# Turning attention outputs by row halves, ahead of the scores instead of behind the attend matmuls

## The chip, the cores and the metric

The kernel runs on one core of a Trainium2 chip. The metric is the device time of one execution in microseconds (us); the median of three runs of the kernel before is 767.42 us (766.53 to 768.09). Engines are named as in the profile: PE is the matmul engine (PEld its weight loads), DVE the vector engine, ACT the scalar engine, POOL the general engine, SP the engine that issues most DMAs.

## The reference: what is computed

Block-sparse attention, then a mixture of experts with one expert per token. Attention has 4 batches, 8 heads, 768 positions and a head size of 64; a mask by blocks of 32 allows neighbours, the first and last block and three sampled blocks per row.

```python
scores = scale * np.matmul(q, k.transpose(0, 1, 3, 2))        # scale = 1 / 8
scores = np.where(mask, scores, -1000000000.0)
attn = np.exp(scores - max); attn = attn / (sum + 1e-09)
out = np.matmul(attn, v)                                       # (4, 8, 768, 64)
x = out.transpose(0, 2, 1, 3).reshape(3072, 512)               # heads side by side
logits = x @ w_gate                                            # 8 experts
# each token goes to its expert of highest logit: y = relu(x @ w1[e]) @ w2[e]
# out = (probability of that expert) * y
```

## The kernel before, in words

**Pairs and steps.** The attention loop (L698) works on 16 pairs of heads; a pair is two heads of one batch, one head on partitions 0 to 63 and one on 64 to 127. Each pair has two steps, one per half of its 768 query rows (384 columns, `CW`, three groups of 128, `HC`), so 32 steps, numbered i from 0. The step (n, half) does, in this order:

- `load` (L87): DMAs of keys, queries and values of pair n+2, when half is 1.
- `turn` (L189): 12 transposes on PE of the keys (half 0) or queries (half 1) of pair n+1 into a PSUM buffer `tp`, and two copies by ACT.
- `scores` (L208), six times: matmuls L216 of keys by queries for both heads, each head from its own 64 partitions, into a PSUM buffer `s`; L219 adds the mask; ACT takes the exponential into `e` (L221); DVE adds the `e` up into `esum` (L227).
- `divide` (L245) for the step before, i-1: matmuls of `esum` by ones (L250, `sp`), ACT copies the sums to `ss` (L252), DVE takes reciprocals in three parts (L257) and multiplies the output `oT` of that step by them (L258).
- `attend` (L229), six times: matmuls L237 of values by `e` into `op`; at the end ACT copies `op` to `oT` (L242), still undivided, with head and dimension on the partitions and query rows on the columns.
- `rows_out` (L260), from n = 1 on, for the pair before, n-1, and the same half. That is the output of step i-2, divided in step i-1. It turns `oT` so that the rows come onto the partitions, and makes this pair's share of the logits, in one go: `oT` is the stationary operand of L270, and the moving one, `mix`, holds for each pair index an identity matrix with 8 columns of `w_gate` beside it (136 columns). Each group of 128 rows goes as two column halves of 64. ACT copies the PSUM tile `xr` to `xb` (L278), DVE adds the logits to `lgn` (L281 or L283), and after the second half SP writes the pair's 128 columns of x to DRAM, `x_rows` (L286). After the last pair of a batch, `gate` (L290) computes the probability of the best expert: DVE, one exponential on ACT, DVE, one small DMA.

From step 25 on, DVE also does the routing of the first three batches (`ranks`, `layout_a`, `one_hots`) and, in step 30, PE a few token matmuls (L593). After the loop come the last `divide`, then 28 expert tiles of two layers (L661, L676), each with its weights fetched by SP into two buffers and its rows gathered by POOL from `x_rows`. The outputs of the last pair are turned there: between the two groups of layer 1 of the first tile (half 0) and behind them (half 1).

**What sets the order.** PE, DVE and POOL run in the order in which the program is written (the manual schedule of L179, until L758). ACT and SP are ordered by the framework's planner. On each engine the work runs one after the other, with semaphores between engines. Buffers: `oT` four, `e` eight, `xb` two; in PSUM, `ps_s` has three buffers of two banks that `tp` and `s` use in turn, `ps_x` one bank for `xr` and `sp`, `ps_o` one for `op`.

Of the kernel before, what the change touches and what calls it, by code (L numbers as in the profile page):

```python
# [7 lines left out]
F32 = mybir.dt.float32  # L8
# [9 lines left out]
def kernel(  # L18
# [11 lines left out]
    nc = tc.nc  # L30
    P = 128
    B, H, S, D = q.shape
# [3 lines left out]
    NCH = S // P  # L36
    CW = NCH // 2 * P
    NPR = H // 2
    N, DM = out.shape
    E = moe_w_gate.shape[1]  # L40
# [17 lines left out]
    ident = const.tile([P, P], F32, name="ident")  # L58
# [4 lines left out]
    wg = const.tile([P, DB, E], F32, name="wg")  # L63
    lgn = const.tile([P, NT, E], F32, name="lgn")
    lmax = const.tile([P, NT], F32, name="lmax")

    x_d = nc.dram_tensor("x_rows", (N, XW), F32, kind="Internal").ap()


    mpool = ctx.enter_context(tc.tile_pool(name="mpool", bufs=1))  # L70
    ps_o = ctx.enter_context(tc.tile_pool(name="ps_o", bufs=1, space=PSUM))
    ps_x = ctx.enter_context(tc.tile_pool(name="ps_x", bufs=1, space=PSUM))

    upper, lent = {}, ExitStack()
# [9 lines left out]
    HC = NCH // 2  # L84
    loaded, turned = {}, {}

    def load(b, pr):  # L87
        got = []
        for src, nm in ((k, "k_sb"), (q, "q_sb")):
            t = ld.tile([P, NCH, 2, D], F32, name=nm)  # L90
            for hh in range(2):

                queue = nc.scalar if nm == "q_sb" and (b, pr) == (0, 0) else nc.sync
                queue.dma_start(t[:, :, hh, :], src[b, 2 * pr + hh].rearrange("(p c) d -> p c d", p=P))
            got.append(t)
        t = ld.tile([P, 2, NCH, D], F32, name="v_sb", bufs=3)
        nc.sync.dma_start(
            t.rearrange("p h c d -> p h (c d)"), v[b, 2 * pr : 2 * pr + 2].rearrange("h (p c) d -> p h (c d)", p=P),
        )
        got.append(t)  # L100
        loaded[(b, pr)] = got
# [2 lines left out]
    oh = mpool.tile([P, NCH, P], BF16, name="oh")  # L104
    pen = mpool.tile([P, S], BF16, name="pen")

    mix = mpool.tile([P, NPR, P + E], F32, name="mix")
    ones = mpool.tile([P, D], F32, name="ones")

    sums = mpool.tile([4 * B * NPR, CW], F32, name="sums")  # L110
# [58 lines left out]

    def make_mix():  # L170
        nc.scalar.dma_start(wg[:], moe_w_gate.rearrange("(c p) e -> p c e", p=P))
        nc.gpsimd.memset(mix[:], 0.0)
        for pr in range(NPR):
            nc.gpsimd.tensor_copy(mix[:, pr, :P], ident[:])
            nc.gpsimd.tensor_copy(mix[:, pr, P:], wg[:, pr, :])

    make_mask_pool = ExitStack()
    by_hand = ExitStack()
# [8 lines left out]
    xpool = ctx.enter_context(tc.tile_pool(name="xpool", bufs=2))  # L187

    def turn(b, pr, which):  # L189

        src = loaded[(b, pr)][which]
        dst = work.tile([P, S], F32, name="qT" if which else "kT")
        turned.setdefault((b, pr), {})[which] = dst
        tp = upper["ps_s"].tile([P, 2, 512], F32, name="tp", tag="s")

        for c in range(NCH):
            for j in range(2):
                r = slice(j * D, (j + 1) * D)
                nc.tensor.transpose(tp[:, j, c * D : (c + 1) * D], src[r, c].rearrange("p h d -> p (h d)"), ident[r, r])  # L199
        for j in range(2):  # L200
            nc.scalar.copy(  # L201
                dst.rearrange("p (c j t) -> p j c t", j=2, t=D)[:, j], tp[:, j, :CW].rearrange("p (c t) -> p c t", t=D),
            )

    rt = {}
    es, ops_, esums, xbs, s_alls = {}, {}, {}, {}, {}

    def scores(n, half, c):  # L208

        b, pr = pairs[n]  # L210
        kT, qT = turned[(b, pr)][0], turned[(b, pr)][1]
        cols = slice(half * CW, (half + 1) * CW)
        s = upper["ps_s"].tile([P, 2, 512], F32, name="s")
        for hh in range(2):
            r = slice(hh * D, (hh + 1) * D)
            nc.tensor.matmul(s[:, hh, :CW], lhsT=kT[r, c * P : (c + 1) * P], rhs=qT[r, cols], start=True, stop=False)  # L216
        for hh in range(2):
            r = slice(hh * D, (hh + 1) * D)
            nc.tensor.matmul(s[:, hh, :CW], lhsT=oh[r, c, :], rhs=pen[r, cols], start=False, stop=True)  # L219
        e = work.tile([P, 2, CW], F32, name="e", bufs=8)  # L220
        nc.scalar.activation(e[:], s[:, :, :CW], AF.Exp, scale=scale)  # L221
        es[(n, half, c)] = e
        if c == 1:
            esums[(n, half)] = work.tile([P, 2, CW], F32, name="esum")
        if c > 0:
            t = esums[(n, half)]
            nc.vector.tensor_add(t[:], es[(n, half, 0)][:] if c == 1 else t[:], e[:])  # L227
# [32 lines left out]
    def rows_out(n, half):  # L260

        b, pr = pairs[n]
        oT = ops_.pop((n, half))
        M = P + E
        xr = ps_x.tile([P, HC, M], F32, name="xr")

        M_ = D if n + 1 < len(pairs) else P
        for m in range(HC):
            for j in range(P // M_):
                nc.tensor.matmul(  # L270
                    xr[j * M_ : (j + 1) * M_, m, :], lhsT=oT[:, m * P + j * M_ : m * P + (j + 1) * M_], rhs=mix[:, pr, :],
                    start=True, stop=True,
                )
        if half == 0:
            xbs[n] = xpool.tile([P, NCH, M], F32, name="xb")
        xb = xbs[n]
        ms = slice(half * HC, (half + 1) * HC)
        nc.scalar.copy(xb[:, ms, :], xr[:])  # L278
        sofar = lgn[:, b * NCH + half * HC : b * NCH + (half + 1) * HC, :]
        if pr == 0:  # L280
            nc.vector.tensor_copy(sofar, xb[:, ms, P:])  # L281
        else:
            nc.vector.tensor_add(sofar, sofar, xb[:, ms, P:])  # L283
        if half == 1:
            rows = x_d[b * S : (b + 1) * S, pr * P : (pr + 1) * P]
            nc.sync.dma_start(rows.rearrange("(p c) w -> p c w", p=P), xb[:, :, :P])  # L286
            if pr == NPR - 1:
                gate(b)

    def gate(b):  # L290
        ts = slice(b * NCH, (b + 1) * NCH)
        nc.vector.reduce_max(lmax[:, ts], lgn[:, ts, :], axis=AX)
        ge = small.tile([P, NCH, E], F32, name="ge", bufs=2)
        nc.vector.tensor_tensor(
            ge[:], lgn[:, ts, :], lmax[:, ts].unsqueeze(2).to_broadcast([P, NCH, E]), op=ALU.subtract,
        )
        nc.scalar.activation(ge[:], ge[:], AF.Exp)
        gs = small.tile([P, NCH], F32, name="gs", bufs=2)
        nc.vector.reduce_sum(gs[:], ge[:], axis=AX)
        nc.vector.tensor_scalar_add(gs[:], gs[:], 1e-9)  # L300
        nc.vector.reciprocal(gs[:], gs[:])
        gw = small.tile([P, NCH, XW - DM], F32, name="gw", bufs=2)
        nc.vector.tensor_copy(gw[:], gs[:].unsqueeze(2).to_broadcast([P, NCH, XW - DM]))
        nc.sync.dma_start(x_d[b * S : (b + 1) * S, DM:].rearrange("(p c) w -> p c w", p=P), gw[:])

    pairs = [(b, pr) for b in range(B) for pr in range(NPR)]
# [141 lines left out]
    def count(ph):  # L448

        cps = bank(ph, [2, E])  # L450
        nc.tensor.matmul(cps[:, 0, :], lhsT=rt["lt"][:], rhs=rt["end" + ph][:], start=True, stop=True)
        nc.tensor.matmul(cps[:, 1, :], lhsT=rt["all"][:], rhs=rt["end" + ph][:], start=True, stop=True)
        cn = rt["cn" + ph] = sm.tile([P, 2, E], F32, name="cn" + ph)
        nc.vector.tensor_copy(cn[:], cps)
# [243 lines left out]
    for i, (n, half) in enumerate(steps):  # L698
        if half == 1 and n + 2 < len(pairs):
            load(*pairs[n + 2])  # L700
        if 0 < i and n + 1 < len(pairs):
            turn(*pairs[n + 1], half)
        for c in range(NCH):
            scores(n, half, c)
        if i == 0:
            make_mix()
        if i == 10:
            route_consts()
        if i > 0:
            divide(*steps[i - 1])  # L710
        for c in range(NCH):
            attend(n, half, c)
        if i == 0:
            turn(*pairs[1], 0)
        if n > 0:
            rows_out(n - 1, half)

        if (n, half) == (NA, 1):
            ranks("A", 0, TA)
        if (n, half) == (NA + 1, 0):  # L720
            count("A")
            layout_a()
            for i_ in range(2):
                fetch(i_, 1)
                fetch(i_, 2)
        if (n, half) == (NA + 1, 1):
            slots_a()
        if n == NA + 2:
            one_hots("A", rt["slA"], TA, KA, half)
        if (n, half) == (NA + 3, 0):  # L730
            tokens("A", TA, KA)
            for i_ in range(3):
                gather(i_)
        if n + 1 == len(pairs) and half == 1:
            turn_x(0)
# [92 lines left out]
```

## Time and profile before

| | us |
|---|---|
| median of three runs | 767.42 |
| the profiled execution's own time | 767.37 |
| its span, first to last instruction | 765.7 |
| start of the scores of step 0, step 1, step 2 | 10.65, 23.14, 33.23 |
| one step in the middle of the loop | 10.78 |
| end of the loop, start of the expert layers | 357.56 |

Busy time in the span: PE 749.5 us, weight loads 475.8, DVE 415.8, ACT 270.2, POOL 67.2. The step in the middle is the distance of two scores' starts in the chain of work that ended last (44.01 to 54.79). A line of the timeline gives the start in us, the busy time, the engine, the line of the kernel, the operation, `out<-in` with the program's names, the shapes, the number of instructions merged into it, and in brackets the idle time of the engine ahead of it and what ended that. Shapes such as 128*64 give rows by columns of the array that a matmul uses; a matmul of f32 shows as two instructions. Matmuls overlap in the pipeline, so the start of the next kind tells more than the end of the last. A line of the windows gives, for one stretch, each engine's busy time, then the TensorE clock granted (1.00 is full speed), the DMA share and GB/s.

### The profile page before, as it was taken

To read this page: it belongs to the slowest core of one execution; us is meant where nothing else is said; L and a number is where in the kernel's file an instruction comes from. 1 tells how busy PE (TensorE), PEld (TensorE's weight loads), DVE (VectorE), ACT (ScalarE), POOL (GpSimd) and SP (SyncE) were. 2 spreads that over 40 slices of the span, in tenths; PEclk is the share of its full clock that TensorE was granted. 3 is DMA by queue.
4 is the path that set the end of the run, shared out by engine and by line. 5 is a ranking of instruction groups with operands and counts; after the bars stand their busy time and mean duration, and the time that the engine had idled before them with its cause. 6 is when DMAs were issued, how large, how long until landed. Compare 5 with 4: busy or idle time off the path is not lost.

```text
span 765.7 us, 13053 instructions
## 1 busy us (share of the span) xinstructions
PE 749.5 (98%) x5134; PEld 475.8 (62%) x5134; DVE 415.8 (54%) x834; ACT 270.2 (35%) x425; POOL 67.2 (9%) x98
## 2 busy tenths in 40 slices
PE   7999999999999999999999999999999999999994
PEld 4555555555555555556777686786776776866682
DVE  4678777777778779997530235533434425323400
ACT  4666676667666675665111000100100100001000
POOL 4000000000000000002011121111111211211010
PEclk8999999999999999999999999999999999999998
DMA  8322333233322331842789989899899899899940
GB/s 187 83 60 48 82 84 85 63 83 84 85 56 51 83 84 44 319 165 78 244 308 333 344 311 348 320 329 346 320 329 362 314 344 345 320 346 339 355 147 6
DMA packets 119362, 157.57 MB, mean 206 GB/s; under 512 B 56499, under 2 KB 72947, under 8 KB 119284
## 3 DMA queue, kind: packets, MB, share of 16 engines
q1 hardware_dynamic: 112672, 142.42, 55.8%
q0 software_dynamic: 4480, 13.75, 4.6%
q8 instruction: 43, 0.70, 0.4%
q10 hardware_dynamic: 2132, 0.41, 0.3%
q14 instruction: 35, 0.29, 0.1%
HBM read 143.79 MB, written 13.73 MB: 206 GB/s over the span
## 4 chain that ended last, share of the span: by engine, by line
PE 86%; DMA 7%; issue 5%; another core or an unknown queue 0%; ACTq 0%; POOL 0%; ACT 0%; DVE 0%; POOLq 0%
PE hp L661 21%; PE zp L676 19%; PE s L216 17%; PE op L237 16%; DMA out_dram<-zo,sB 6%; PE s L219 4%; PE sp L250 3%; PE xr L270 3%; PE tp L199 2%; DMA q_sb<-in_q_dram 1%; PE tpg L650 0%; POOL xg L620 0%; ACT qT L201 0%; ACTq L117 0%
## 5 line engine op out<-in xcount | busy, mean ns | idle before, releaser
L661 PEld LDWEIGHTS hp<-xgT,w 128*128 128x128 f32 x1792 | 204.7, 192 | 12.6 <-issue 8.6
L661 PE MATMUL hp<-xgT,w 128*128 128x128 f32 x1792 | 205.6, 275 | 0.0
L676 PE MATMUL zp<-w,hT 128*128 128x512 f32 x448 | 196.9, 593 | 0.0
L642 DVE STREAM_TRANSPOSE xgT<-xg 32x128 f32<-32x128 f32 x352 | 106.5, 303 | 110.0 <-DMA xg<-x_rows,gB 94.0
L216 PE MATMUL s<-qT,kT 64*128 64x384 f32 x768 | 159.2, 493 | 0.9 <-ACT qT L201 0.9
L221 ACT ACTIVATE e<-s 128x768 f32<-128x768 f32 x192 | 152.4, 812 | 7.0 <-PE s L219 5.2
L676 PEld LDWEIGHTS zp<-w,hT 128*128 128x128 f32 x448 | 83.0, 190 | 94.2 <-issue 94.2
L227 DVE TENSOR_TENSOR esum<-esum,e 128x768 f32<-128x768 f32 x128 | 122.7, 958 | 14.6 <-ACT e L221 1.1
L237 PE MATMUL op<-e,v_sb 128*64 128x384 f32 x768 | 129.3, 486 | 0.0
L237 PEld LDWEIGHTS op<-e,v_sb 128*64 128x64 f32 x768 | 55.1, 137 | 68.8 <-issue 68.8
L216 PEld LDWEIGHTS s<-qT,kT 64*128 64x128 f32 x768 | 67.1, 190 | 38.4 <-issue 33.5
L257 DVE RECIPROCAL r<-ss 128x128 f32<-128x128 f32 x96 | 82.2, 912 | 1.3 <-ACT ss L252 1.3
L668 ACT ACTIVATE hT<-hp 128x512 f32<-128x512 f32 x33 | 19.7, 597 | 177.4 <-PE hp L661 174.4
L681 ACT ACTIVATE zo<-zp,xg 128x512 f32<-128x512 f32 x28 | 19.2, 687 | 176.7 <-PE zp L676 176.7
L666 DVE TENSOR_SCALAR hT<-hp 128x512 f32<-128x512 f32 x23 | 15.9, 692 | 101.4 <-issue 57.9
L227 DVE TENSOR_TENSOR esum<-e 128x768 f32<-128x768 f32 x32 | 30.6, 957 | 63.2 <-ACT e L221 63.2
L219 PE MATMUL s<-pen,oh 64*128 64x384 bf16 x384 | 63.2, 326 | 0.0
L242 ACT COPY oT<-op 128x384 f32<-128x384 f32 x32 | 15.3, 479 | 106.2 <-PE op L237 106.2
L682 POOL DMA_INDIRECT out_dram<-zo,sB x23 | 23.3, 1013 | 259.7 <-ACT zo L681 259.7
L219 PEld LDWEIGHTS <-oh 64*128 64x128 bf16 x384 | 18.9, 95 | 25.8 <-issue 0.9
L270 PEld LDWEIGHTS xr<-mix,oT 128*64 128x64 f32 (+1 forms) x372 | 24.0, 139 | 10.7 <-issue 10.7
L250 PE MATMUL sp<-esum,ones 128*64 128x384 f32 x128 | 27.7, 512 | 0.0
(174 smaller groups left out, 260.1 us busy)
## 6 DMA issues: line engine op xcount, KB each, us to landing
w<-in_moe_w_dram SPq DMA_DIRECT2D x56, 2048.0 KB
k_sb<-in_k_dram SPq DMA_DIRECT2D x32, 192.0 KB
v_sb<-in_v_dram SPq DMA_DIRECT2D x16, 384.0 KB
x_rows<-xb SPq DMA_DIRECT2D x16, 384.0 KB
q_sb<-in_q_dram SPq DMA_DIRECT2D x30, 192.0 KB
sums<-ss SPq DMA_DIRECT2D x32, 3.0 KB
q_sb<-in_q_dram ACTq DMA_DIRECT2D x2, 192.0 KB
xg<-x_rows,gB POOLq DMA_INDIRECT x23, 7.5
```

What stands on the lines that cost most here:

```text
L216: nc.tensor.matmul(s[:, hh, :CW], lhsT=kT[r, c * P : (c + 1) * P], rhs=qT[r, cols], start=True, stop=False)
L219: nc.tensor.matmul(s[:, hh, :CW], lhsT=oh[r, c, :], rhs=pen[r, cols], start=False, stop=True)
L221: nc.scalar.activation(e[:], s[:, :, :CW], AF.Exp, scale=scale)
L227: nc.vector.tensor_add(t[:], es[(n, half, 0)][:] if c == 1 else t[:], e[:])
L237: nc.tensor.matmul(op[hh * D : (hh + 1) * D, :], lhsT=v_sb[:, hh, c, :], rhs=e[:, hh, :], start=(c == 0), stop=(c == NCH - 1),)
L250: nc.tensor.matmul(sp[hh * D : (hh + 1) * D, :], lhsT=ones[:], rhs=esum[:, hh, :], start=True, stop=True)
L257: nc.vector.reciprocal(r[:, m * P : (m + 1) * P], ss[:, m * P : (m + 1) * P])
L270: nc.tensor.matmul(xr[j * M_ : (j + 1) * M_, m, :], lhsT=oT[:, m * P + j * M_ : m * P + (j + 1) * M_], rhs=mix[:, pr, :], start=True, stop ...
L642: nc.vector.transpose(xT[d, :, t], xg[t, :DM].rearrange("p (c q) -> p c q", c=DB)[:, :, d])
L661: nc.tensor.matmul(hp[:, m, :], lhsT=st[i]["w1"][:, c, fb * P : (fb + 1) * P], rhs=st[i]["xT"][:, c, :], start=(c == 0), stop=(c == DB - 1),)
L676: nc.tensor.matmul(zp[:], lhsT=st[i]["hT"][:, fb, :], rhs=st[i]["w2"][:, fb, :], start=(fb == 0), stop=(fb == FB - 1),)
L682: ins = nc.gpsimd.indirect_dma_start(out=out[:, :], out_offset=bass.IndirectOffsetOnAxis(ap=of("s", i, P), axis=0), in_=zo[:], in_offset=N ...
```

## The change

`rows_out` moves from the end of step (n, half) to its start, ahead of `turn` and the scores; it still serves pair n-1 and the same half. For all pairs but the last, L270 is split by row halves: for each group of 128 rows and each head, 64 partitions of `oT` (one head) times 64 partitions of a smaller `mix` (64x64 identity and that head's 64 rows of `w_gate`, 72 columns). The two heads write to two banks of a `ps_s` buffer, `xr2`. ACT copies it in one instruction (432 elements per partition instead of 408). The logits now come in two shares, added by two DVE instructions, and the rows go to DRAM by two DMAs per pair, one per head, with pieces of 64 numbers instead of 128. The last pair keeps its place in the expert layers, whole groups of 128 columns and a table of its own, `mix2`. `make_mix` fills the smaller tables.

```diff
     def make_mix():
         nc.scalar.dma_start(wg[:], moe_w_gate.rearrange("(c p) e -> p c e", p=P))
-        nc.gpsimd.memset(mix[:], 0.0)
         for pr in range(NPR):
-            nc.gpsimd.tensor_copy(mix[:, pr, :P], ident[:])
-            nc.gpsimd.tensor_copy(mix[:, pr, P:], wg[:, pr, :])
+            for hh in range(2):
+                r = slice(hh * D, (hh + 1) * D)
+                nc.gpsimd.tensor_copy(mix[r, pr, :D], ident[r, r])
+            nc.gpsimd.tensor_copy(mix[:, pr, D:], wg[:, pr, :])
+        nc.gpsimd.tensor_copy(mix2[:, :P], ident[:])
+        nc.gpsimd.tensor_copy(mix2[:, P:], wg[:, NPR - 1, :])
...
+            W = D + E
+            xr = upper["ps_s"].tile([P, 2, 512], F32, name="xr2", tag="s")
+            for m in range(HC):
+                for hh in range(2):
+                    r = slice(hh * D, (hh + 1) * D)
+                    nc.tensor.matmul(
+                        xr[:, hh, m * W : (m + 1) * W], lhsT=oT[r, m * P : (m + 1) * P], rhs=mix[r, pr, :], start=True, stop=True,
+                    )
+            xb = xbs[n].rearrange("p (h c w) -> p h c w", h=2, c=NCH)
+            nc.scalar.copy(xb[:, :, ms, :], xr[:, :, : HC * W].rearrange("p h (c w) -> p h c w", c=HC))
+            for hh in range(2):
+                part = xb[:, hh, ms, D:]
+                if pr == 0 and hh == 0:
+                    nc.vector.tensor_copy(sofar, part)
+                else:
+                    nc.vector.tensor_add(sofar, sofar, part)
+                if half == 1:
+                    nc.sync.dma_start(dest[:, :, hh * D : (hh + 1) * D], xb[:, hh, :, :D])
...
     for i, (n, half) in enumerate(steps):
         if half == 1 and n + 2 < len(pairs):
             load(*pairs[n + 2])
+
+        if n > 0:
+            rows_out(n - 1, half)
         if 0 < i and n + 1 < len(pairs):
             turn(*pairs[n + 1], half)
         for c in range(NCH):
...
             attend(n, half, c)
         if i == 0:
             turn(*pairs[1], 0)
-        if n > 0:
-            rows_out(n - 1, half)
```

More of the change, by code (lines that the diff above doesn't have):

```diff
@@ L105 @@
     pen = mpool.tile([P, S], BF16, name="pen")
-    mix = mpool.tile([P, NPR, P + E], F32, name="mix")
+    mix = mpool.tile([P, NPR, D + E], F32, name="mix")
+    mix2 = mpool.tile([P, P + E], F32, name="mix2")
     ones = mpool.tile([P, D], F32, name="ones")
@@ L263, in rows_out @@
         oT = ops_.pop((n, half))
[L264 to L273, printed above, removed]
-        if half == 0:
-            xbs[n] = xpool.tile([P, NCH, M], F32, name="xb")
@@ L276, in rows_out @@
[L276 to L281, printed above, removed]
-        else:
-            nc.vector.tensor_add(sofar, sofar, xb[:, ms, P:])
+        ms = slice(half * HC, (half + 1) * HC)
+        sofar = lgn[:, b * NCH + half * HC : b * NCH + (half + 1) * HC, :]
+        if half == 0:
+            xbs[n] = xpool.tile([P, 2 * NCH * (D + E)], F32, name="xb")
@@ new lines, in rows_out @@
+        dest = x_d[b * S : (b + 1) * S, pr * P : (pr + 1) * P].rearrange("(p c) w -> p c w", p=P)
+        if n + 1 == len(pairs):
+            xr = ps_x.tile([P, HC, P + E], F32, name="xr")
+            for m in range(HC):
+                nc.tensor.matmul(xr[:, m, :], lhsT=oT[:, m * P : (m + 1) * P], rhs=mix2[:], start=True, stop=True)
+            xb = xbs[n][:, : NCH * (P + E)].rearrange("p (c w) -> p c w", c=NCH)
+            nc.scalar.copy(xb[:, ms, :], xr[:])
+            nc.vector.tensor_add(sofar, sofar, xb[:, ms, P:])
+            if half == 1:
+                nc.sync.dma_start(dest, xb[:, :, :P])
+        else:
+            W = D + E
+            xr = upper["ps_s"].tile([P, 2, 512], F32, name="xr2", tag="s")
+            for m in range(HC):
+                for hh in range(2):
[11 more added lines that the diff above has]
+                    nc.vector.tensor_add(sofar, sofar, part)
+                if half == 1:
+                    nc.sync.dma_start(dest[:, :, hh * D : (hh + 1) * D], xb[:, hh, :, :D])
@@ L284, in rows_out @@
         if half == 1:
-            rows = x_d[b * S : (b + 1) * S, pr * P : (pr + 1) * P]
-            nc.sync.dma_start(rows.rearrange("(p c) w -> p c w", p=P), xb[:, :, :P])
             if pr == NPR - 1:
```

## The prediction, made before the result was known

> **What bounds the kernel now.** I read the chain of work that ended last first, then the timeline of one step of the attention loop by engine, then the waits.
>
> ```profile
> PE 86%; DMA 7%; issue 5%; another core or an unknown queue 0%; ACTq 0%; POOL 0%; ACT 0%; DVE 0%; POOLq 0%
> ```
>
> The chain runs on PE almost throughout: any time in which PE stands still in the attention loop is added to the end. The loop has 32 steps, one about every 10.78 us. Here is PE in step 11 (its scores begin at 130.11) and at the seam to step 12 (140.89), then two rows of the weight loads:
>
> ```profile
> 130.11 0.86 PE L216 MATMUL s<-qT,kT 64*128 64x384 f32 x4
> ...
> 135.10 0.87 PE L250 MATMUL sp<-esum,ones 128*64 128x384 f32 x4
> 135.80 4.04 PE L237 MATMUL op<-e,v_sb 128*64 128x384 f32 x24
> 139.67 0.86 PE L270 MATMUL xr<-mix,oT 128*64 128x136 f32 x12
> 140.47 0.58 PE L199 MATMUL tp<-ident,k_sb 64*128 64x64 f32 x12
> 140.89 0.86 PE L216 MATMUL s<-qT,kT 64*128 64x384 f32 x4
> ```
> ```profile
> 140.46 0.45 PEld L199 LDWEIGHTS tp<-ident,k_sb 64*128 64x128 f32 x12 [0.18 <-issue]
> ...
> 141.59 0.35 PEld L216 LDWEIGHTS s<-qT,kT 64*128 64x128 f32 x4 [0.23 <-issue]
> ```
>
> PE goes from one kind to the next without a hole: scores 4.99 us (130.11 to 135.10), sums 0.70, attend 3.87, outputs 0.80, turned keys 0.42; together 10.78. Now DVE and ACT over the same stretch:
>
> ```profile
> 130.17 0.56 DVE L258 TENSOR_TENSOR oT<-oT,r 128x384 f32<-128x384 f32 x1
> ...
> 132.89 0.96 DVE L227 TENSOR_TENSOR esum<-e 128x768 f32<-128x768 f32 x1 [2.07 <-ACT e L221]
> 133.95 4.15 DVE L227 TENSOR_TENSOR esum<-esum,e 128x768 f32<-128x768 f32 x4
> 138.01 2.57 DVE L257 RECIPROCAL r<-ss 128x128 f32<-128x128 f32 x3
> 140.62 0.56 DVE L258 TENSOR_TENSOR oT<-oT,r 128x384 f32<-128x384 f32 x1
> ```
> ```profile
> 131.24 4.79 ACT L221 ACTIVATE e<-s 128x768 f32<-128x768 f32 x6
> 136.02 0.49 ACT L252 ACTIVATE ss<-sp 128x384 f32<-128x384 f32 x1
> 139.89 0.48 ACT L242 COPY oT<-op 128x384 f32<-128x384 f32 x1 [3.38 <-PE op L237]
> 140.58 0.50 ACT L278 COPY xb<-xr 128x408 f32<-128x408 f32 x1 [0.22 <-PE xr L270]
> 141.09 0.86 ACT L201 COPY kT<-tp 128x384 f32<-128x384 f32 x2
> ```
>
> The multiply of L258 in this step ends at 140.62 + 0.56 = 141.18. It divides the output of step 10 (divide is called for the step before). The matmuls of L270 at 139.67 don't need it: they turn the output of step 9, divided at 130.17 + 0.56 = 130.73, which gives 8.9 us of room. That room is why PE never waits for a division:
>
> ```profile
> PEld xr L270 <- issue: 10.7, 60, 0.2
> ```
>
> In the list of waits this is the only entry of L270: never DVE.
>
> **Which output is turned at a seam.** Step i ends with rows_out of step i-2 before the change. After it, step i begins with rows_out of step i-2. Nothing lies on PE between the end of one step and the start of the next, so PE does the same kinds in the same order (attend, outputs, turned keys, scores); but the output that is turned is one step younger. At the seam of 139.67 it is that of step 10, whose multiply ends at 141.18. The stationary operand of the new matmul is oT, so the first weight load of xr2 waits: PE could begin at 139.67 and may begin at 141.18. Behind that load stand the 12 transposes of the keys and all scores of the next step; ACT has nothing to exponentiate and DVE nothing to add until they come.
>
> **The new length of a step.** With PE waiting for DVE, DVE for ACT and ACT for PE, the step is a loop, which I walk from the first exponential (e0).
> - e0 to the end of the multiply: 131.24 to 141.18 = 9.94 us (two exponentials, five adds at 1.03 to 1.06, three reciprocals, the multiply). The division before the change goes through the same: nothing here is touched.
> - End of the multiply to the first weight load: I take 0.05, from ACT's copy ending at 141.95 and its next one beginning 0.01 later at the one end, and 0.2 (the "issue" gap of the L270 row) at the other.
> - Weight load to first matmul: 0.16 (L216: 141.59 in the loads, 141.75 on PE).
> - First output matmul to the next e0, as it is now: 139.67 to 141.09 + 0.86 = 141.95, so 2.28.
> - What the new shape changes in that: 12 matmuls stream 72 columns instead of 136, but load 64x128 weights instead of 128x64. No row shows this pair. By streaming alone the 0.69 of the chain's xr piece would fall by 72/136 to 0.37; by the loads of the transposes (12 of the same size in 0.45 us) also about 0.4; by L216's (four in 0.35 us, each about 0.19, two row halves beside each other, so about 0.115 per pair) 6 x 0.115 = 0.69. L216's is the nearest row, a full f32 multiply from the same halves, so I take 0.69: no change. ACT's copy has 432 elements instead of 408, by 479 ns for 384 and 499 for 408 about 0.02 more; the last, shorter matmul ends 0.05 earlier. Together 2.26.
>
> Sum: 9.94 + 0.05 + 0.16 + 2.26 = 12.41 us, against 10.78: **1.63 us more per step**.
>
> **The whole loop.** Step 2 is the first with a turned output at its start. Step 1 had none on PE, so there the matmuls themselves are new as well: the multiply of step 1 ends at 34.18 and the exponentials of step 2 began at 34.13.
>
> ```profile
> 33.62 0.56 DVE L258 TENSOR_TENSOR oT<-oT,r 128x384 f32<-128x384 f32 x1
> ```
>
> e0 of step 2 moves to 34.18 + 2.47 = 36.65, 2.5 us later. Steps 3 to 29 are 27 times 1.63 = 44.0. Steps 30 and 31 have no keys to turn; there e0 waits for the first scores, not for ACT's copies, and the old steps were 10.35 and 10.95 (the second holds 0.6 of token matmuls, which now lie in the stall); I estimate 1.6 and 1.0. Step 31 no longer ends with an output: 0.79 back (xr at 355.23, the next transposes at 356.02). 2.5 + 44.0 + 2.6 - 0.8 = 48.3. The gate of a batch (DVE, ACT, DVE: its exponential stood between the two key copies and made e0 0.15 us late unnoticed) falls into the loop three times: 0.6. Sum 48.9.
>
> **What is hidden.** One more add of logits per step (0.18) lies in DVE's idle time ahead of the next exponentials (2.07 now, some 3.7 then); uncovered it would be 30 x 0.2 = 6. The new tables are 14 copies on POOL (64x64 or 128x8, at most 0.29 each, so 4 us once) instead of a memset and 8 copies, more than 10 us ahead of their first use. The 15 further row transfers take SP 0.59 each; the bytes are the same in pieces half as long. SP's key loads behind them are issued some 40 us (141.78 against a turn at about 183) ahead of need, so I charge nothing, at worst 15 x 0.59 = 9 if SP were the bound. One xr2 buffer more goes round in the three of ps_s: the second scores of a step need its copy, which ends 0.86 ahead of e0. The routing work on DVE (up to 2.4 us after a multiply in steps 25 to 29) fits ahead of the next e1, which comes 4.1 us after it. The second half, from 357 us on, only starts later. It streams its weights through two buffers, so a longer loop prefetches nothing more.
>
> **The clock.** PE will stand for about 1.4 us in each step. The only holes that this trace shows are ahead of 10.65 us, the longest 2.6 us, and the clock fell after them:
>
> ```profile
> 8.00:10.00 2.00, 1.20 (x22) 0.90 (x18) 0.84 (x2) 1.12 (x3) 0.89 (x6) 0.71 1.37 216
> ...
> 14.00:16.00 2.00, 2.00 (x12) 1.08 (x12) 0.90 (x1) 0.96 (x2) 0.00 (x0) 0.58 1.27 222
> ```
>
> The seventh figure is the granted clock: 0.71 means half speed from 8.84, 0.58 until 15.68, so 6.8 us. [...] No row here has a hole of 1.4 us at full clock, so it stays a rival.
>
> **The rivals.** (1) *Not slower*: DVE divides ahead of its adds. The sums are copied at 136.02 + 0.49 = 136.51; three reciprocals and the multiply behind that end at 139.7, just when PE arrives. Then there is no wait, and the time is 767 if the matmuls cost the same, 757 if they fall from 0.69 to 0.37 (30 x 0.32). It decides from the point where the multiply ends 1.5 us earlier in the step. Against it: DVE takes its work in the written order in this step, the first reciprocal coming only after the fifth add although its input was there 1.5 us before. That the turned output in effect stays where it was, because the order isn't what I read, would give 767 too. (2) *The clock falls at each stall.* At half speed outputs and keys take 1.1 more and two rounds of scores 1.6 more (0.81 now), so about 3 us per step: 30 x 3 on top is about 906; at some stalls only, from 840 up. (3) *Dear loads*: the two row halves don't load beside each other. L661 loads 32 full weights in 3.57 us, 0.111 each; 12 x 0.111 = 1.33 instead of 0.69, which is 30 x 0.64 = 19 more: 836. At the other end the transposes' loads give 30 x 0.27 = 8 less: 808.
>
> **How the numbers follow.** The profiled execution took 767.37 (its span 765.7 and 1.7 around it), the median is 767.42: 767.4 + 48.9 = **816**. Forecast 0.85 (803 to 832: loads, wake-up 0.05 to 0.2, DVE's further add). Dear loads 0.03, the clock 0.07, not slower 0.05, of it 0.03 faster and 0.02 the same. The range 803 to 834 leaves out the clock and the not slower case and most of the dear loads. Faster, same and slower by over 0.2%, about what a measurement of this kernel can tell from no change: 0.03, 0.02, 0.95.
>
> **What would show it.** Right: a wait of PEld at xr2 for DVE's oT, some 30 times with about 1.5 us each; steps of 12.4 us; DVE's idle time ahead of esum up by 1.6; clock 1.0 throughout; xr2 about 0.7 long, and the second half as long as before. Wrong: no such wait (rival 1), slices at a lower clock (rival 2), an xr2 stretch of 0.4 or 1.3 us (loads).

## The result and the profile after

The changed kernel takes 814.25 us (median of 6 runs, 813.52 to 814.85) against 767.23 in the same runs before: a ratio of 1.0612, interval 1.0598 to 1.0626. The prediction was 816, in a range of 803 to 834. The profiled execution has a span of 811.8 us, 46.1 more than before; the expert layers start at 403.7 us instead of 357.6, so all of it lies ahead of them, in the attention loop.

The chain of work that ended last, by engine, of the changed kernel:

```profile
PE 50%; DVE 22%; issue 16%; DMA 6%; ACT 4%; POOL 1%; another core or an unknown queue 0%; DVEq 0%; POOLq 0%
```

DVE had 0% of it before and now has 22%, PE 50% instead of 86%. The waits of the changed kernel (waiter, what it waited for: total us, times, longest):

```profile
PEld xr L290 <- issue: 58.5, 28, 2.3
...
PE xr L290 <- DVE oT L262: 38.1, 27, 1.7
```

This is the seam, the join of two steps on PE: 27 times PE waits 1.41 us, and what ends the wait is the multiply. The weight loads' own row names no releaser ("issue"); it counts the time since the last load of attend. (The three other seams wait as well, 0.7, 1.4 and 1.4 us, and name a routing instruction of DVE that stands behind the multiply.) One seam by engine; line numbers are 4 to 20 higher than before:

```profile
151.82 4.04 PE L241 MATMUL op<-e,v_sb 128*64 128x384 f32 x24
157.28 0.89 PE L290 MATMUL xr<-mix,oT 64*128 64x72 f32 x12 [1.42 <-DVE oT L262]
157.97 0.57 PE L203 MATMUL tp<-ident,k_sb 64*128 64x64 f32 x12
158.34 0.90 PE L220 MATMUL s<-qT,kT 64*128 64x384 f32 x4
```
```profile
157.25 0.78 PEld L290 LDWEIGHTS xr<-mix,oT 64*128 64x128 f32 x12 [2.06 <-issue]
```
```profile
153.97 2.57 DVE L261 RECIPROCAL r<-ss 128x128 f32<-128x128 f32 x3
156.57 0.56 DVE L262 TENSOR_TENSOR oT<-oT,r 128x384 f32<-128x384 f32 x1
158.76 0.40 DVE L300 TENSOR_TENSOR lgn<-lgn,xb 128x24 f32<-128x24 f32 x2 [1.63 <-ACT xb L294]
```
```profile
147.19 4.85 ACT L225 ACTIVATE e<-s 128x768 f32<-128x768 f32 x6
...
158.20 0.52 ACT L294 COPY xb<-xr 128x432 f32<-128x432 f32 x1 [1.82 <-PE xr L290]
158.62 0.87 ACT L205 COPY kT<-tp 128x384 f32<-128x384 f32 x2
159.44 4.85 ACT L225 ACTIVATE e<-s 128x768 f32<-128x768 f32 x6
```

The multiply ends at 157.13, PE's first matmul follows at 157.28, and a step, from one e0 (147.19) to the next (159.44), is 12.25 us. DVE, which PE waits for, then stands idle itself for 1.63 us, until ACT has copied the outputs: the engines wait for each other in a ring.

Two steps were longer than the others, 13.8 and 13.6 us. Windows of the changed kernel over step 9 and step 10 (busy time of PE, PEld, DVE, ACT, POOL, then the granted clock, DMA share, GB/s):

```profile
119.80:132.20 12.40, 10.73 (x92) 5.92 (x90) 9.37 (x17) 6.77 (x13) 0.00 (x0) 1.00 0.43 99
132.30:146.10 13.80, 12.47 (x94) 6.74 (x91) 8.36 (x13) 7.00 (x12) 1.11 (x7) 0.88 0.13 31
```

A clock of 0.88 over 13.8 us is half speed for 3.3 us. In the profiled execution it happened at two seams of 30.

### The profile page after: what moved, and what is told of

It is laid out like the page before. It is cut to its first block, busy times and chain, and to the rows that moved or that the text cites. A ratio compares the mean times of both kernels' runs of the same rounds, so it can differ in the third digit from the quotient of the medians.

```text
span 811.8 us, 13112 instructions
## 1 busy us (share of the span) xinstructions
PE 753.6 (93%) x5134; PEld 487.0 (60%) x5134; DVE 422.0 (52%) x864; ACT 267.1 (33%) x425; POOL 66.9 (8%) x103
## 4 chain that ended last, share of the span: by engine, by line
PE 50%; DVE 22%; issue 16%; DMA 6%; ACT 4%; POOL 1%; another core or an unknown queue 0%; DVEq 0%; POOLq 0%
PE hp L678 14%; PE s L220 13%; PE zp L693 13%; DVE esum L231 10%; DVE r L261 9%; DMA out_dram<-zo,sB 6%; PE xr L290 3%; ACT e L225 3%; PE s L223 3%; DVE oT L262 2%; PE tp L203 1%; PE op L241 1%; POOL xg L637 1%; DVE allow L152 0%; PE tpg L667 0%
## 5 line engine op out<-in xcount | busy, mean ns | idle before, releaser
L220 PE MATMUL s<-qT,kT 64*128 64x384 f32 x768 | 162.0, 498 | 1.1 <-ACT qT L205 1.1
L220 PEld LDWEIGHTS s<-qT,kT 64*128 64x128 f32 x768 | 74.0, 192 | 33.6 <-issue 29.4
L223 PE MATMUL s<-pen,oh 64*128 64x384 bf16 x384 | 69.4, 327 | 0.0
L290 PE MATMUL xr<-mix,oT 64*128 64x72 f32 x360 | 26.9, 279 | 41.6 <-DVE oT L262 38.1
L290 PEld LDWEIGHTS xr<-mix,oT 64*128 64x128 f32 x360 | 23.4, 187 | 59.6 <-issue 58.5
L223 PEld LDWEIGHTS <-oh 64*128 64x128 bf16 x384 | 25.1, 96 | 20.4 <-issue 1.6
```

Of the source, the lines that this page charges most:

```text
L290: nc.tensor.matmul(xr[:, hh, m * W : (m + 1) * W], lhsT=oT[r, m * P : (m + 1) * P], rhs=mix[r, pr, :], start=True, stop=True,)
```

## The experiments

Each changes one thing of the changed kernel (of the kernel before, for e2; e5 also changes the number of two buffers). Ratios are to runs of the kernel before on the same chip, at 767.28 us for e1 to e4 and 766.84 for e5 to e8.

**e1: the shape without the place.**

```diff
-        if n > 0:
-            rows_out(n - 1, half)
         if 0 < i and n + 1 < len(pairs):
...
         if i == 0:
             turn(*pairs[1], 0)
+        if n > 0:
+            rows_out(n - 1, half)
```

> The new shape alone: row halves, xr2 in ps_s, two row DMAs per pair, two logit adds, but rows_out at the end of the step as before the change, so that a seam turns the output that is one step older. Theory (the whole loss is PE waiting for the multiply of an output that is one step too young): no wait of xr2 for DVE, steps of 10.7 to 10.8 us, 764 to 770 in all. Rival (the shape costs: 128-column loads, the shared ring of ps_s, the longer ACT copy, shorter DMA pieces): 775 or more, up to 814 if it is all of it.

Measured: 767.09 us, ratio 0.9996 (0.9987 to 1.0005); steps of 10.76 us, no wait of xr2 for DVE. The shape is neutral where it is.

**e2: the place without the shape.** The same move of two lines made in the kernel before.

> The new place alone: the kernel before with rows_out moved to the start of the step, whole 128-column identity, ps_x buffer, one row DMA. Theory: the same wait of about 1.4 us at each of 30 seams, steps of 12.2 to 12.4 us, 810 to 819 in all. Rival (the shape costs): under 790.

Measured: 817.2 us, ratio 1.0652 (1.0636 to 1.0669); steps of 12.43 us. Its waits:

```profile
PE xr L270 <- DVE oT L258: 38.5, 27, 1.7
```

The place alone is the whole loss, and a little more. With the new shape a waiting step is 0.18 us shorter; 0.15 of it lies in ACT's copies, where xb to e0 took 159.96 to 161.35 here and 158.20 to 159.44 in the changed kernel.

**e3: divide ahead of the scores.** Place and shape stay.

```diff
+        if i > 0:
+            divide(*steps[i - 1])
         for c in range(NCH):
             scores(n, half, c)
...
-        if i > 0:
-            divide(*steps[i - 1])
         for c in range(NCH):
             attend(n, half, c)
```

> The changed kernel with divide of the step before called ahead of the scores instead of behind them, so that DVE's reciprocals and multiply come before the five adds and are done some 5 us before the next seam. Place and shape stay those of the change. Theory: the wait is gone; PE changes between row and column halves twice more per step, each about 0.1 us by the seams of before: 766 to 776. Rival (the buffers, ACT's order of copies or the shape hold PE at the seam): 800 or more.

Measured: 783.08 us, ratio 1.0211 (1.0196 to 1.0227). The regular wait is gone, as expected, but the total missed by 7. Steps are 11.05 us, not 10.76, and one step had a hole of 3.7 us on PE; the scores behind it took 1.49 to 1.65 us a round instead of 0.81. PE's row and ACT's row name that hole's cause:

```profile
339.63 1.65 PE L220 MATMUL s<-qT,kT 64*128 64x384 f32 x4 [3.71 <-ACT e L225]
```
```profile
338.38 0.49 ACT L256 ACTIVATE ss<-sp 128x384 f32<-128x384 f32 x1 [4.93 <-DMA sums<-ss]
```

The small DMA of the sums (3 KB) took 9.35 us, from 328.95 to 338.30, and held an `ss` buffer until then. In the execution before the change, where four loads of expert weights of 2 MB each are issued from 308.28 to 313.08, the DMA engines' busy share is 1.03 from 313 to 330 us, and the same DMA held ACT for 1.7 us; DVE's reciprocals waited 1.3 us for it and PE not at all. That the loads held it up in e3 too is my reading.

**e5: divide first in the step**, so that the sums' matmuls lie between attend and the outputs.

```diff
-            oT = work.tile([P, CW], F32, name="oT", bufs=4)
+            oT = work.tile([P, CW], F32, name="oT", bufs=3)
...
-        ss = work.tile([P, CW], F32, name="ss")
+        ss = work.tile([P, CW], F32, name="ss", bufs=3)
...
+        if i > 0:
+            divide(*steps[i - 1])
         if n > 0:
             rows_out(n - 1, half)
...
-        if i > 0:
-            divide(*steps[i - 1])
         for c in range(NCH):
             attend(n, half, c)
```

> The changed kernel with divide of the step before called first of all in the step, so that PE's order at a seam is attend, sums, outputs, keys, scores: the reciprocals come ahead of the adds as in the kernel that divides ahead of the scores, but the sums' matmuls (column halves) stand next to the attend matmuls (column halves). Three buffers for ss and three for oT instead of two and four, so that a late sums DMA can't hold ACT. Theory (in the kernel that divides ahead of the scores, the 0.29 us left per step came from its two further changes between row and column halves, and its one hole of 3.7 us from the sums DMA): steps of 10.7 to 10.8 us, no hole in the loop, 765 to 771. Rival (the 0.29 is the sums' matmuls or ACT's longer list at the seam): steps of 11.0 or more, 775 to 785.

Measured: 774.40 us, ratio 1.0094 (1.0078 to 1.0109). Steps are 10.76 us, so e3's 0.29 went with the two further changes between column and row halves (in neither kernel does PE wait in such a step). The total missed by 3: the three steps with a gate took 12.2 to 12.4, and those with routing on DVE about 11.5. DVE, ACT and PE at a gate:

```profile
109.73 2.58 DVE L261 RECIPROCAL r<-ss 128x128 f32<-128x128 f32 x3 [2.09 <-ACT ss L256]
112.42 0.56 DVE L262 TENSOR_TENSOR oT<-oT,r 128x384 f32<-128x384 f32 x1
...
113.56 0.21 DVE L311 TENSOR_TENSOR ge<-lgn,lmax 128x48 f32<-128x48 f32 x1
...
114.85 0.95 DVE L231 TENSOR_TENSOR esum<-e 128x768 f32<-128x768 f32 x1
```
```profile
111.26 0.81 ACT L225 ACTIVATE e<-s 128x768 f32<-128x768 f32 x1
113.80 0.24 ACT L314 ACTIVATE ge<-ge 128x48 f32<-128x48 f32 x1 [1.73 <-DVE ge L311]
113.95 3.64 ACT L225 ACTIVATE e<-s 128x768 f32<-128x768 f32 x5
```
```profile
114.80 0.92 PE L220 MATMUL s<-qT,kT 64*128 64x384 f32 x4 [1.15 <-ACT e L225]
```

Here the gate's exponential waits for DVE, which is busy dividing, and five exponentials wait behind it on ACT; PE's scores stop for 1.15 us.

**e4: the division twice.**

```diff
-        for m in range(HC):
+        for m in [*range(HC), *range(HC)]:
             nc.vector.reciprocal(r[:, m * P : (m + 1) * P], ss[:, m * P : (m + 1) * P])
```

> The changed kernel with each of the three reciprocals of a step taken twice (the same result), 2.57 us more on DVE per step between the last add and the multiply. Theory: the step is a loop through DVE, so the 30 seams wait 2.57 us more each, 4.0 us per hole: 814 + 77 = 891 if the clock stays as it is. In the changed kernel the granted clock fell for 3.4 us after two of the three holes of 1.67 us and after none of 1.42 us; if a hole's length within the clock's window decides, it falls at every seam now, and outputs, keys and the first scores take twice as long for 3.4 us: 1.4 to 1.7 more per step, 930 to 945. Rival (DVE is not in the loop): under 840.

Measured: 954.6 us (two runs). Most holes are 3.6 to 4.1 us, most steps 16.2 to 17.3. 12.25 + 2.57 would be 14.82; the other 2.3 us are the clock. On the page:

```profile
PEclk9877878878788887887978899999999999999998
```

At 27 seams of 30, behind holes of 3.8 us in the mean, it fell for 6.83 us, not for the 3.4 that I had reckoned with, which is why the time passed 945. The mean granted clock is 0.894, against 0.992 in the changed kernel.

**e6: one reciprocal twice.**

```diff
-        for m in range(HC):
+        for m in [*range(HC), 0]:
```

> The changed kernel with one reciprocal of the three taken twice: 0.86 us more on DVE per step, holes of 2.28 us. Theory without the clock: 814 + 26 = 840 or less. With the clock: a hole of 1.67 us inside one clock window lowered it and one of 1.42 did not, and with 3.85 us it fell at every seam for 2.3 us each; at 2.28 us about 7 seams in 10 leave 1.65 us or more inside one window of 3.41 us, which adds 30 x 0.7 x 1.5 to 2.3, so 870 to 890. If the clock falls at no seam or at every seam (905 or more), the window is not what decides.

Measured: 883.0 us (two runs, 878.3 and 887.7), inside the range that reckons with the clock. In the profiled one the clock fell at 21 seams of 30, the 7 in 10 that were expected, and its mean was 0.937. That a stretch of 3.41 us decides, by the idle time within it, was my estimate: the count agrees with it, but no run here shows it by itself. Two stretches of 15.5 us without and with a fall:

```profile
102.00:117.50 15.50, 11.12 (x90) 5.99 (x88) 11.35 (x16) 7.46 (x12) 0.00 (x0) 1.00 0.28 69
117.50:133.00 15.50, 14.04 (x88) 7.79 (x88) 8.57 (x12) 7.14 (x11) 0.00 (x0) 0.78 0.14 34
```

**e7 and e8: the last one or two adds behind the division.** Only DVE's order changes; PE's stays that of the change. This is e8; e7 has `NCH - 1` in place of `NCH - 2`.

```diff
             t = esums[(n, half)]
-            nc.vector.tensor_add(t[:], es[(n, half, 0)][:] if c == 1 else t[:], e[:])
+            if c < NCH - 2:
+                nc.vector.tensor_add(t[:], es[(n, half, 0)][:] if c == 1 else t[:], e[:])
...
         if i > 0:
             divide(*steps[i - 1])
+        for c in range(NCH - 2, NCH):
+            t = esums[(n, half)]
+            nc.vector.tensor_add(t[:], t[:], es[(n, half, c)][:])
```

> The changed kernel with the last of the five adds of a step placed behind the division on DVE. Place, shape and PE's order stay those of the change. Theory: the multiply ends 1.06 us earlier in the step, so the holes shrink from 1.42 to 0.36 us: steps of 11.2 us and no fall of the clock, 778 to 785. Rival (DVE is not what PE waits for): 810 or more.

Measured e7: 782.58 us, ratio 1.0197 (1.0182 to 1.0213); holes of 0.41 us, steps of 11.24, no fall of the clock in the waiting steps.

> The changed kernel with the last two adds of a step placed behind the division on DVE, which is the point from which the prediction's first rival decides: the division then starts when the sums are there, and the multiply ends some 9.6 us after the scores began, just when PE arrives. Theory: no hole over 0.2 us, steps of 10.76 to 10.9 us, 765 to 774. If a wait remains that the adds don't explain: 790 or more.

Measured e8: 772.28 us, ratio 1.0063 (1.0050 to 1.0077); steps of 10.85. DVE and PE of e8 at a seam:

```profile
148.72 2.58 DVE L262 RECIPROCAL r<-ss 128x128 f32<-128x128 f32 x3 [0.58 <-ACT ss L257]
151.33 0.56 DVE L263 TENSOR_TENSOR oT<-oT,r 128x384 f32<-128x384 f32 x1
151.81 1.94 DVE L734 TENSOR_TENSOR esum<-esum,e 128x768 f32<-128x768 f32 x2
```
```profile
152.03 0.89 PE L291 MATMUL xr<-mix,oT 64*128 64x72 f32 x12
```

Now the reciprocals wait for the sums instead of following the last add. The multiply ends at 151.89 and PE goes on at 152.03: the two meet, as the first rival had it. The 5 us that stay are in the main 0.07 per step (2 us), a hole of 1.3 at the very end, where the last sums wait for the deferred adds, and longer steps where DVE does routing.

Undone by place (e1) the loss is gone, undone by DVE's order (e8) all but 5 us of it; kept by place alone (e2), it stays. No version here beats the kernel before beyond its interval: with PE full, a step is 10.76 to 10.78 us in every order that neither waits nor changes more often between row and column halves.

## Why the prediction was right, and where its sizes were off

The mechanism was right: the turned output is one step too young, PE waits for its multiply, and the step becomes a ring. By its own terms:

| term | predicted | measured |
|---|---|---|
| e0 to the end of the multiply | 9.94 | 9.94 |
| multiply to the first weight load | 0.05 | 0.12 (157.13 to 157.25) |
| load to first matmul | 0.16 | 0.03 |
| first output matmul to the next e0 | 2.26 | 2.16 (157.28 to 159.44) |
| a step | 12.41 | 12.25 |
| scores of step 1 to those of step 2 | +2.5 | +2.3 (12.40 against 10.09) |
| the 27 steps up to step 29 | +44.0 | +43.6 (334.81 against 291.25) |
| steps 30 and 31 | +2.6 | +2.45 |
| the last seam | -0.8 | -0.8 |
| ahead of step 1 | 0 | -1.4 |
| sum | 48.9 (with gates 0.6) | 46.1 |

- **The ring.** Its largest part was read from rows that the change leaves alone, and held to the hundredth. The load waits longer after the multiply than I took, but the matmul, with PE idle ahead of it, follows in 0.03; together 0.15 instead of 0.21. ACT's copy of the outputs overlaps the next copy: 0.42 us from one start to the next, where the old shape took 0.51.
- **The loads.** Taking the scores' row was right: 12 loads in 0.78 us, 0.69 from the first output matmul to the keys. Neither the short stream nor the dear loads came.
- **27 steps.** That 44.0 and 43.6 agree so well is partly luck: 27 x 1.47 is 39.7. The other 3.9 are gates and the clock: each gate made its step 0.25 longer (0.6 foreseen for all three), and the two falls cost about 3, which the sum had at nothing.
- **The clock.** I gave its fall 0.07 in all, at each stall (906) or at some (from 840 up), and expected 1.0 throughout. It came, but at two seams: gates lengthened the holes there from 1.42 to 1.67 us (the gate's exponential runs on ACT ahead of e0, which came 12.62 us after the one before instead of 12.25), and the step after took 1.6 and 1.4 us more. So the price of "some stalls" was wrong: about 3 us, not the 24 and more that 840 means. That the sum has no term for the clock rested on no run, since no row of before has such a hole in the loop; in the changed kernel the clock stayed at 1.00 behind the holes of 1.42 us.
- **Hidden costs.** The second logit add, the tables, the 15 further DMAs and the shared ring of ps_s cost nothing, as charged: e1 has them all at 0.9996.
- **The first rival.** Its point was right: e8 ends the multiply early enough, and the wait is gone. Its price was nearly right: 767 if the matmuls cost the same, as they do, against 772, where e8's own later adds cost some of the 5.
- **Ahead of step 1** 1.4 us went that I had not thought of: 0.3 ahead of the first scores, and step 0 took 11.25 us instead of 12.33. That is the clock at the start of the execution: in both executions the first round of scores took 1.65 us and the last of step 0 0.81, full speed began at 13.18 us here and at 15.66 before the change, and step 0 is 9.83 us plus half of its time ahead of that, within 0.01. The mean clock of the kernel before goes from 0.991 to 0.997 between its own executions, so it varies without any change; what sets the start of full speed stays open. So the sum came so near partly by luck: this gain and the falls of the clock, neither of them in the sum, have opposite signs.

## What to carry to other kernels

When a piece of a software pipeline moves across a seam between steps, first ask which step's data it serves there: here the order of kinds on PE was the same, and one step less of lead turned 8.9 us of room into a wait of 1.4. The price of such a wait is read off the other engine's rows, and the loop through all engines gives the new step length better than the engine's share of busy time. A short, regular hole may also cost clock (here holes of 1.42 us never did, two of three of 1.67 us did), so its length is worth knowing to a few tenths.

## What the runs showed of the hardware

- **The granted clock.** In the changed kernel's loop it was at half speed twice, from 132.65 to 136.06 and from 231.64 to 235.05, 3.41 us each; the two falls and the start of full speed at 13.18 lie whole multiples of 3.413 us apart (the falls 29). PE's holes ahead of them were 1.67 and 1.68 us and ended at 131.19 and 231.02. Behind the holes of 1.42 us, behind one of 1.60 (to 32.95) and behind a third of 1.67 (to 330.95) it stayed at 1.00. Counted on from these changes in stretches of 3.413 us, the first two holes lie within one stretch each, the third across two, with 1.35 and 0.32. In e6, with holes of 2.2 us in the mean, the clock fell at 21 seams of 30; in e4, with 3.8, at 27. What decides a fall stays open: no run here separates the length of a hole from its place or from the work around it.
- **How long a fall lasts.** 3.41 us in the changed kernel; 6.83 us at 27 seams of e4, and also in the execution before the change (8.83 to 15.66), ahead of which PE had stood for 2.60 us. What sets the length stays open too.
- **Changes between row and column halves.** e3 and e5 have the same matmuls; e3 has two more such changes per step and takes 11.05 instead of 10.76 us, so about 0.15 each, as an estimate from that difference.
